# Second layer of an MLP as a Strassen product, in rounds of four feature pairs

## The chip, the cores and the metric

The kernel runs on one core of a Trainium2 chip. The metric is the device time of one execution in microseconds, lower is better, as the median of three runs. One execution was also taken by the hardware profiler; its page and its trace are what is read below.

## The reference

An attention block over 8 x 8 heads gives a matrix of 4352 tokens by 512. Two MLPs follow, one on the result of the other, all in float32:

```
x = attention(x, state)          # 4352 x 512
h = x @ w_in                     # 512 -> 2048
g = where(h >= 1, h, where(h <= -1, 0, (h + 1)**2 / 4))
x = g @ w_out                    # 2048 -> 512
h = x @ w2_in                    # 512 -> 2048
g = max(h, 0) + alpha * min(h, 0)
out = g @ w2_out                 # 2048 -> 512
```

The change concerns the last three lines.

## The kernel before

Every float32 matrix is split in two parts, a high part (a cast on ScalarE, `hi_`, line 73) and a low part (a subtraction on VectorE, `lo_`, line 76). A product of two matrices is three TensorE products, high by high, high by low and low by high.

The first part of the kernel runs the attention and the first MLP together, in 144 steps (nine token tiles by sixteen feature blocks). A table `side` holds, for each step, what else is to be issued there: loads, the decoding of the weights, and the preparation of the second MLP. `decode` takes a weight tile that was loaded as 8-byte numbers and packs it to float32 by one operation on ScalarE and four on VectorE. The decoded `w2_in` goes to memory as it is (`wid`), the decoded `w2_out` as its high and low part (`wod`).

The second MLP is `second()`. The tokens are cut into five superblocks (`HALF`), each of two halves `tk`, the halves 512 tokens wide in the first two superblocks and 384 in the others. Layer 1 takes, for a superblock, two feature blocks at a time (a unit `q`; eight units for a superblock, forty in all). It is a Strassen product (in Winograd's form): the 2 x 2 blocks of features by inner dimension, and of inner dimension by tokens, are multiplied by seven block products instead of eight, `h_item`, line 759, six TensorE products each. Sums of weight blocks (`w_sums`, line 661) and of x blocks (`x_sums`, line 726) are formed before, sums of the results after (`h_after`, line 784). `slope` (lines 768 and 770) then applies the activation. The weights of a unit are fetched raw (`wr_get`, line 646), summed and split again for each superblock.

Layer 2 is the plain product: `o_item`, line 824, one feature block at a time, with g as the stationary operand, 128 tokens of it, and 512 columns of `w2_out` moving. Each token tile of 128 has an accumulator of its own, which takes all sixteen feature blocks, so the result has tokens on its partitions, is copied once and stored by one transfer. `wo_get`, line 744, fetches the split weights of a feature block anew for each half.

The order in `second()` is a merged list: layer-1 products in their order, and a layer-2 item m at place 36 + 1.75 m. `run` and the framework's scheduler turn the program's order into each engine's order; instructions of one engine then run in the order that stands in the program. Tiles come from two pools: U tiles of 2 KB per partition (80 of them) and V tiles of 4 KB (10). PSUM has eight banks, four for accumulators (`pa`) and four for the rest (`pp`). Nearly all loads and stores are issued by the queue of SyncE (SP).

Of the kernel before, what the change touches and what calls it, by code (L numbers as in the profile page):

```python
# [40 lines left out]
def kernel_body(ctx: ExitStack, tc: tile.TileContext, x, state, w1i, w1o, w2i, w2o, alpha, out):  # L41
    nc = tc.nc
    up = ctx.enter_context(tc.tile_pool(name="up", bufs=80))
# [52 lines left out]
    wid = dp.tile([8, 2, 128, 512], F32, name="wid")  # L96
    wod = dp.tile([NF, 128, 1024], F32, name="wod")
# [536 lines left out]
    WR, WU, WB = {}, {}, {}  # L634
# [4 lines left out]
    def w2i_store(j, kh):  # L639
        ld.dma_start(out=wid[j, kh], in_=G.pop(("dec", ("w2i", j, kh))))  # L640

    def wr_get(q):

        for kh in range(2):
            t = U(f"wr{q}{kh}")
            ld.dma_start(out=t, in_=wid[q % 8, kh])
            WR[q, kh] = t

    def parts(t):
        return t.rearrange("p (k e c) -> p k e c", k=2, e=2)  # L650

    def w_sums(q):
        r0, r1 = [parts(WR[q, kh]) for kh in range(2)]
        a11, a21, a12, a22 = r0[:, :, 0], r0[:, :, 1], r1[:, :, 0], r1[:, :, 1]
        sa, sb = U(f"sa{q}"), U(f"sb{q}")
        WR[q, 2], WR[q, 3] = sa, sb
        va, vb = parts(sa), parts(sb)
        s2, s1, s3, s4 = va[:, :, 0], va[:, :, 1], vb[:, :, 0], vb[:, :, 1]
# [5 lines left out]
    def w_split(q, n):  # L664

        t, h = WR.pop((q, n)), U(f"wh{q}{n}", F32R)
        if n == 0:
            t = parts(t)[:, :, 0]
            h, l = [h[:, v * 256:(v + 1) * 256].rearrange("p (k c) -> p k c", k=2) for v in range(2)]
        else:  # L670
            l = U(f"wl{q}{n}", F32R)
        hi_(h, t)
        yield
        yield
        lo_(l, t, h)
        if n == 0:
            WU[q, 0] = h, l
            return
        h, l = parts(h), parts(l)
        for e, k in enumerate({1: (1, 3), 2: (5, 4), 3: (6, 2)}[n]):  # L680
            WU[q, k] = (h[:, :, e], l[:, :, e])

    def pairs(j):
        return 2 * j, 2 * j + 1

    FO = list(range(NF))

    def w2o_put(n):

        raw = G.pop(("dec", ("w2o", FO[n])))  # L690
        h, l = U(f"woh{n}", F32R), U(f"wol{n}", F32R)
        hi_(h, raw)
        WR["o", n] = h, l
        yield
        lo_(l, raw, h)

    def w2o_store(n):
        for e, t in enumerate(WR.pop(("o", n))):
            ld.dma_start(out=wod[FO[n], :, e * 512:(e + 1) * 512], in_=t.bitcast(F32))
# [6 lines left out]
    HO = [0, 5, 4, 6, 1, 2, 3]  # L706
    XR, XB, XT, HB, GT, GR, GS, OA = {}, {}, {}, {}, {}, {}, {}, {}
# [20 lines left out]
    def x_prep(s, step):  # L728

        w = wof(s)  # L730
        n = HO[step]
# [10 lines left out]
    def wo_get(m):  # L742
        t = V(f"wv{m}", F32R)
        ld.dma_start(out=t.bitcast(F32), in_=wod[FO[m % NF]])
        WB["o", m] = t

    def h_item(n):
        q, k = divmod(n, 7)
        s, p = q // 8, HO[k]
        bank = {0: "A", 1: "A", 5: "D", 6: "D", 3: "D", 4: "E", 2: "E"}[p]  # L750
        if p in (0, 5, 4):
            HB[q, bank] = PS(f"hB{q}{p}")
        ps = HB[q, bank][:, :wof(s)]
        wh, wl = WU.pop((q, p))
        m = 0
        for kk in range(2):
            xh, xl = XB[s, p, kk]
            for a, b in ((wh, xh), (wh, xl), (wl, xh)):
                pe.matmul(ps, a[:, kk], b, start=(p in (0, 5, 4) and m == 0), stop=(m == 5),  # L759
                          skip_group_check=True)  # L760
                m += 1

    def slope(q, e, tk, h, g=None):

        s, w = q // 8, wof(q // 8)
        f = pairs(q % 8)[e]
        m = U(f"m{q}{e}{tk}")[:, :w]
        act.activation(out=m, in_=h, func=AF.Relu, scale=-1.0)  # L768
        g = GR[2 * s + tk, f] = m if g is None else g
        dve.scalar_tensor_tensor(out=g, in0=m, scalar=beta_sb[:, f:f + 1], in1=h, op0=ALU.mult, op1=ALU.add)  # L770

    def h_after(n):

        q, k = divmod(n, 7)
        w = wof(q // 8)
        p = HO[k]
        A, D, E = [HB[q, b][:, :w] if (q, b) in HB else None for b in "ADE"]

        def tmp(name):
            GT[q, name] = U(f"{name}_{q}")[:, :w]  # L780
            return GT[q, name]

        def plus(out, a, b):
            dve.tensor_tensor(out=out, in0=a, in1=b, op=ALU.add)  # L784
            return out

        if p == 0:
            act.copy(tmp("p1"), A)
        elif p == 5:
            plus(tmp("u2"), D, GT[q, "p1"])  # L790
        elif p == 1:
            slope(q, 0, 0, A)
        elif p == 6:
            h = plus(tmp("u3"), D, GT[q, "p1"])
            plus(h, E, h)
            slope(q, 1, 1, h, h)
        elif p == 3:
            h = plus(GT[q, "p1"], D, GT[q, "p1"])
            slope(q, 1, 0, h, h)
        elif p == 2:  # L800
            h = plus(GT[q, "u2"], E, GT[q, "u2"])
# [294 lines left out]
```

## Time and profile before

| | |
|---|---|
| median of three runs | 1432.91 us (1432.69 to 1433.84) |
| span of the profiled execution, first to last instruction | 1429.7 us |
| its own time beside the span | not recorded apart; the median of the runs is 3.2 us above the span |
| TensorE, VectorE, ScalarE busy | 98%, 73%, 55% |
| granted TensorE clock | 0.998 of full speed |
| moved by DMA | 253.43 MB, mean 177 GB/s |

Busy time is a sum of instruction times without their overlap. TensorE's instructions are pipelined, so a busy TensorE may still not be at its peak; the distance between the starts of two products tells what one costs. The chain that ended last is followed back from the last instruction, at each step to what released it.

### The profile page before, as it was taken

What the parts mean: (1) busy time and instruction counts of PE and PEld (TensorE: products, weight loads), DVE (VectorE), ACT (ScalarE), POOL (GpSimd) and SP (SyncE); (2) the same over time, 40 slices, a digit from 0 to 9 for tenths busy, and PEclk for the clock granted to TensorE, in tenths of its full rate; (3) what the DMA queues carried; (4) which work ended last, traced back from release to release, by engine and by line L of the source; (5) the groups of instructions that cost most, each with busy time, mean ns of one, the idle gap of its engine ahead of it and who ended that gap; (6) DMA issues with size and microseconds to landing.
All of it is one profiled execution on the core that took longest, in us unless ns stands there. A gap on an engine that the chain in (4) does not pass through costs nothing.

```text
span 1429.7 us, 18991 instructions
## 1 busy us (share of the span) xinstructions
PE 1405.3 (98%) x6548; PEld 1170.0 (82%) x6548; DVE 1044.2 (73%) x1884; ACT 784.4 (55%) x1502; POOL 91.2 (6%) x94
## 2 busy tenths in 40 slices
PE   6799999999999999999999999999999999999998
PEld 4466688888888888888988888888888899989987
DVE  7888685868787888763789786659666976786742
ACT  5566676776776777764644353335433544454431
POOL 1000001121100000000200110002000200010000
PEclk9999999999999999999999999999999999999999
DMA  6898415788744554565323453354545555664545
GB/s 210 309 319 298 119 52 155 212 225 226 216 155 140 162 163 133 163 213 182 120 89 103 155 185 127 125 177 162 177 138 190 201 186 178 201 210 163 184 167 201
DMA packets 146793, 253.43 MB, mean 177 GB/s; under 512 B 47240, under 2 KB 59784, under 8 KB 146696
## 3 DMA queue, kind: packets, MB, share of 16 engines
q1 hardware_dynamic: 107560, 234.54, 49.1%
q0 software_dynamic: 33280, 8.51, 3.2%
q10 hardware_dynamic: 5856, 9.18, 1.7%
q8 instruction: 51, 0.84, 0.3%
q14 instruction: 46, 0.38, 0.1%
HBM read 195.96 MB, written 55.57 MB: 176 GB/s over the span
## 4 chain that ended last, share of the span: by engine, by line
PE 89%; DVE 6%; DMA 2%; ACT 1%; issue 1%; ACTq 0%; SPq 0%; DVEq 0%
PE accB L824 24%; PE accA L613 21%; PE hB L759 21%; PE hA L84 13%; PE accA L605 3%; PE vgp L84 1%; PE sr L84 1%; PE sc L84 1%; DMA vr<-vd 1%; DVE xt L726 1%; DVE gs L76 1%; DMA vd<-vgo 1%; DVE xl L76 1%; PE et L198 0%; DMA wr_wi<-in_moe_w_in_dram 0%
## 5 line engine op out<-in xcount | busy, mean ns | idle before, releaser
L824 PE MATMUL accB<-wv,gs 128*128 128x512 f32 x1632 | 397.2, 391 | 0.0
L824 PEld LDWEIGHTS accB<-wv,gs 128*128 128x128 f32 x1632 | 305.1, 188 | 59.3
L759 PE MATMUL hB<-xh,wh 128*128 128x384 f32 (+1 forms) x640 | 216.9, 359 | 1.0 <-DVE u L784 0.9
L759 PE MATMUL hB<-xl,wh 128*128 128x384 f32 (+1 forms) x560 | 200.2, 357 | 0.0
L759 PE MATMUL hB<-xh,wl 128*128 128x384 f32 (+1 forms) x480 | 170.9, 358 | 0.0
L581 DVE SCALAR_TENSOR_TENSOR g<-y,hA 128x512 f32<-128x512 f32 (+1 forms) x144 | 94.0, 653 | 65.3 <-ACT y L579 64.9
L759 PEld LDWEIGHTS hB<-xh,wh 128*128 128x128 f32 x640 | 119.5, 188 | 17.4 <-DVE u L784 3.3
L578 ACT ACTIVATE y<-hA 128x512 f32<-128x512 f32 (+1 forms) x144 | 82.5, 573 | 87.4 <-PE hA L84 86.1
L768 ACT ACTIVATE m<-u 128x384 f32<-128x384 f32 (+1 forms) x80 | 45.4, 568 | 134.5 <-DVE u L784 134.4
L76 DVE TENSOR_TENSOR gl<-g,gh 128x512 fp32r<-128x512 f32 (+1 forms) x128 | 93.0, 726 | 31.6 <-ACT gh L73 29.7
L759 PEld LDWEIGHTS hB<-xl,wh 128*128 128x128 f32 x560 | 105.1, 188 | 12.6
L76 DVE TENSOR_TENSOR gs<-u,gs 128x384 fp32r<-128x384 f32 (+1 forms) x80 | 48.6, 609 | 72.5 <-ACT gs L73 72.1
L759 PEld LDWEIGHTS hB<-xh,wl 128*128 128x128 f32 x480 | 90.0, 188 | 7.6
L73 ACT CAST gh<-g 128x512 fp32r<-128x512 f32 (+1 forms) x128 | 75.6, 591 | 28.6 <-DVE g L581 26.8
L579 ACT ACTIVATE y<-y 128x512 f32<-128x512 f32 (+1 forms) x144 | 87.6, 608 | 4.3
L73 ACT CAST gs<-u 128x384 fp32r<-128x384 f32 (+1 forms) x80 | 44.4, 556 | 82.0 <-PE accB L824 80.9
L784 DVE TENSOR_TENSOR u<-hB,p 128x384 f32<-128x384 f32 (+1 forms) x80 | 48.5, 607 | 40.9 <-PE hB L759 40.8
L770 DVE SCALAR_TENSOR_TENSOR u<-m,beta_sb,u 128x384 f32<-128x384 f32 (+1 forms) x80 | 56.0, 700 | 25.1 <-ACT m L768 24.2
L605 PE MATMUL accA<-g,wf_w1o 128*128 128x512 f32 x128 | 60.7, 607 | 4.6 <-DVE wf_w1o L398 4.6
L493 ACT COPY vgo<-vgp 128x512 f32<-128x512 f32 x64 | 37.2, 585 | 43.0 <-PE vgp L84 21.9
L76 POOL TENSOR_TENSOR xl<-xr,xh 128x384 fp32r<-128x384 f32 (+1 forms) x15 | 18.4, 1225 | 621.4 <-ACT xh L73 621.4
L73 ACT CAST wh<-sa 128x512 fp32r<-128x512 f32 x40 | 24.8, 621 | 56.7 <-DVE sa L661 51.1
(960 smaller groups left out, 3063.5 us busy)
## 6 DMA issues: line engine op xcount, KB each, us to landing
wv<-wod SPq DMA_DIRECT2D x160, 512.0 KB
wr<-wid SPq DMA_DIRECT2D x80, 256.0 KB
vd<-vgo SPq DMA_DIRECT2D x64, 256.0 KB
x<-in_x_dram SPq DMA_DIRECT2D x30, 512.0 KB
vr<-vd SPq DMA_DIRECT2D x56, 256.0 KB
out_dram<-oB SPq DMA_DIRECT2D x33, 256.0 KB
wr_wi<-in_moe_w_in_dram SPq DMA_DIRECT2D x16, 512.0 KB
wr_w1o<-in_moe_w_out_dram SPq DMA_DIRECT2D x16, 512.0 KB
```

Of the source, the lines that this page charges most:

```text
L73: act.copy(h, raw)
L76: (eng or dve).tensor_tensor(out=l, in0=raw, in1=h.bitcast(F32), op=ALU.subtract)
L84: pe.matmul(ps, a, b, start=(k == 0), stop=(k == n - 1))
L578: act.activation(out=y[:, :n], in_=ps, func=AF.Relu, bias=0.5, scale=0.5)
L579: act.activation(out=y[:, :n], in_=y[:, :n], func=AF.Square)
L581: dve.scalar_tensor_tensor(out=g[:, :n], in0=y[:, :n], scalar=1.0, in1=ps, op0=ALU.min, op1=ALU.max)
L605: pe.matmul(ACC[k], w[:, k * 128:(k + 1) * 128], g, start=(f == 0), stop=(f == NF - 1))
L613: pe.matmul(ACC[k][:, :n], a, b, start=(f == 0 and j == 0), stop=(f == NF - 1 and j == 2))
L759: pe.matmul(ps, a[:, kk], b, start=(p in (0, 5, 4) and m == 0), stop=(m == 5), skip_group_check=True)
L770: dve.scalar_tensor_tensor(out=g, in0=m, scalar=beta_sb[:, f:f + 1], in1=h, op0=ALU.mult, op1=ALU.add)
L784: dve.tensor_tensor(out=out, in0=a, in1=b, op=ALU.add)
L824: pe.matmul(OA[k], a, b, start=(r == 0 and j == 0), stop=(r == NF - 1 and j == 2))
```

## The change

Layer 2 becomes a Strassen product too. A round `r` takes one half superblock of features: four feature pairs `jj` (units 4r to 4r + 3), so two rounds for each superblock, ten in all. For each of the seven products `p` the four pairs are added up in one bank, for each of two column halves `cc` of 128 output features. The weights are now the stationary operand and g moves, 512 or 384 tokens at a time. Three chains of products share the banks: products 0, 5, 6, 3 go on adding in one bank, and after each product the state of the bank is one block of the result and is read out (`o_after`: a copy in the first round, a sum with the copy in the second); 4 and 2 share another, 1 has its own. Layer 1 takes the same chains (`h_item`, `h_after`).

The result stands with output features on the partitions. `o_turn` turns it by 32 x 32 blocks on VectorE, four blocks into one tile, and stores it in pieces of 32 partitions by 4 x 128 columns.

The sums of blocks of g are formed in `o_prep`, in place where possible. The sums of weight blocks of both layers are formed and split once, and stored (`w1c`, 7 products for 8 pairs, and `w2c`): in the first part of the kernel for `w2_in` and for the first two pairs of `w2_out`, and within `second()`, in its first 63 places, for the other six pairs. `second()` fetches one tile for a layer-1 product (`w1_get`, six products ahead) and one V tile for two layer-2 items (`w2_load`, four items ahead). The order: layer-1 products one by one, layer-2 item m at place 34.5 + m. The preparation of x for the next superblock is spread over two units. There are 82 U tiles; the tile `stT` moves from a place of its own to the pool of V tiles.

The core of the diff, of the new side (the old functions stand above):

```diff
-    up = ctx.enter_context(tc.tile_pool(name="up", bufs=80))
+    up = ctx.enter_context(tc.tile_pool(name="up", bufs=82))
...
+    A_CHAIN, B_CHAIN, C_CHAIN = (0, 5, 6, 3), (4, 2), (1,)
+    ORDER = A_CHAIN + B_CHAIN + C_CHAIN
...
+    def w_sums(key, a11, a21, a12, a22, shape):
+        sa, sb = U(f"sa{key[0]}{key[1]}"), U(f"sb{key[0]}{key[1]}")
+        s2, s1, s3, s4 = [shape(t[:, h:h + 256]) for t in (sa, sb) for h in (0, 256)]
...
         for o, a, b, op in ((s1, a21, a22, ALU.add), (s2, s1, a11, ALU.subtract),
                             (s3, a11, a21, ALU.subtract), (s4, a12, s2, ALU.subtract)):
             dve.tensor_tensor(out=o, in0=a, in1=b, op=op)
             yield
...
+    def w_split(key, *products):
+        shape = w1_shape if key[0] == "i" else w2_shape
+        for p in products:
+            src = WS[key].pop(p)
+            t = U(f"ws{key[0]}{key[1]}{p}", F32R)
+            hi_(shape(t[:, :256]), src)
+            yield
+            lo_(shape(t[:, 256:]), src, shape(t[:, :256]))
...
+    L1 = []
+    for q in range(8 * NSUP + 1):
+        for k, (d, p) in enumerate(((0, 0), (1, 4), (0, 5), (1, 2), (0, 6), (1, 1), (0, 3))):
+            if 0 <= q - d < 8 * NSUP:
+                L1.append((q, k, q - d, p))
+    L2 = [(r, p, jj) for r in range(2 * NSUP) for p in ORDER for jj in range(4)]
...
+    def h_after(q, p):
...
+        if p in (0, 5, 6):
+            act.copy(g, ps)
         elif p == 3:
+            slope(q, e, g, ps)
+        else:
+            dve.tensor_tensor(out=g, in0=ps, in1=g, op=ALU.add)
+            slope(q, e, g, g)
...
+    def o_prep(m):
...
+        src = {0: b11, 5: b11, 6: b12, 4: b11, 2: b22, 1: b21}.get(p)
+        if p == 5:
+            dve.tensor_tensor(out=b12, in0=b22, in1=b12, op=ALU.subtract)
+            dve.tensor_tensor(out=b11, in0=b12, in1=b11, op=ALU.add)
+        elif p == 3:
+            src = U(f"t4{q}")[:, :w]
+            dve.tensor_tensor(out=src, in0=b21, in1=b11, op=ALU.subtract)
+        elif p == 4:
+            dve.tensor_tensor(out=b11, in0=b22, in1=b11, op=ALU.subtract)
         v = V(f"gs{m}", F32R)
...
+        hi_(h, src)
+        lo_(l, src, h)
...
     def o_item(m):
+        r, p, jj = L2[m]
...
+        for cc in range(2):
+            if p in (0, 4, 1) and jj == 0:
+                OA[cc, p] = pa.tile([128, 512], F32, tag="acc", name=f"o{r}{p}{cc}")
+            ps = OA[cc, 0 if p in A_CHAIN else 4 if p in B_CHAIN else 1][:, :w]
+            wh, wl = [t[:, h + cc * 128:h + cc * 128 + 128] for h in (0, 256)]
+            for k, (a, b) in enumerate(((wh, gh), (wh, gl), (wl, gh))):
+                pe.matmul(ps, a, b, start=(p in (0, 4, 1) and jj == 0 and k == 0), stop=(jj == 3 and k == 2),
+                          skip_group_check=True)
+            if jj == 3:
+                o_after(r, p, cc, ps)
...
+    def o_after(r, p, cc, ps):
...
+        if p in A_CHAIN and not last:
+            OC[key] = U(f"c{s}{hh}{tk}{cc}")[:, :w]
+            act.copy(OC[key], ps)
+        else:
+            dve.tensor_tensor(out=OC[key], in0=ps, in1=OC[key], op=ALU.add)
+        if last and p in (3, 4, 2, 1):
+            o_turn(s, hh, tk, cc, OC.pop(key))
+
+    def o_turn(s, hh, tk, cc, c):
...
+            dve.transpose(out=o[:, :4 * n].rearrange("p (j k x) -> p k j x", k=4, x=32)[:, k],
+                          in_=c[:, v:v + n].rearrange("p (j t) -> p j t", t=32))
...
+                for i in range(4):
...
+                    ld.dma_start(out=dst[:, :, i * 128:(i + 1) * 128],
+                                 in_=o[32 * i:32 * i + 32, 4 * u:4 * u + 512].rearrange("p (j c) -> p j c", j=4))
...
-        LAG = 36
...
+        LAG = 34.5
+        ev = [(n, 0, n) for n in range(len(L1))] + [(LAG + m, 1, m) for m in range(len(L2))]
+        later = defaultdict(list)
+        for j in range(2, 8):
+            n = 6 + 9 * (j - 2) if j < 4 else 35 + 7 * (j - 4)
+            later[n - 4].append((w2_get, j))
+            later[n].append((w2_sums, j))
+            for k in range(4):
+                later[n + 1 + k].append((w_split, ("o", j), *ORDER[2 * k:2 * k + 2]))
+                later[n + 3 + k].append((w_store, ("o", j), *ORDER[2 * k:2 * k + 2]))
...
+                w1_get(n + AW)
...
+                w2_load(n + 4)
+                o_prep(n + 2)
                 o_item(n)
...
-            at(o + 4, w2i_store, *key[1:])
...
+        elif key[2]:
+            at(o + 2, w1_sums, key[1])
+            for k in range(4):
+                at(o + 3 + k, w_split, ("i", key[1]), *ORDER[2 * k:2 * k + 2])
+                at(o + 5 + k, w_store, ("i", key[1]), *ORDER[2 * k:2 * k + 2])
...
+    AW = 6
...
-    stT["t"] = cp.tile([128, 1024], F32, name="stT")
+    stT["t"] = V("stT")
```

## Rows read from the trace of the kernel before

**Rows 1.** The page's busy times: us, share of the span, instructions.

```profile
PE 1405.3 (98%) x6548; PEld 1170.0 (82%) x6548; DVE 1044.2 (73%) x1884; ACT 784.4 (55%) x1502; POOL 91.2 (6%) x94
```

**Rows 2.** The chain that ended last: start us, us, what; second MLP and end.

```profile
879.13 2.72 PE hB L759 x12
881.85 2.72 PE accB L824 x12
...
1360.54 2.10 PE hB L759 x12
1362.64 2.08 PE accB L824 x9
...
1382.53 42.90 PE accB L824 x189
1425.45 0.38 ACT oB L832
1425.85 0.42 DVE oB L833
```

**Rows 3.** Windows: us, busy of each engine (instructions), TensorE clock, DMA share, GB/s.

```profile
280.00:300.00 20.00, 20.00 (x96) 16.76 (x95) 13.72 (x27) 14.06 (x27) 3.76 (x4) 1.00 0.88 227
...
550.00:600.00 50.00, 50.00 (x237) 41.87 (x236) 45.14 (x87) 34.13 (x66) 0.00 (x0) 1.00 0.40 121
...
765.00:1000.00 235.00, 234.85 (x1040) 194.66 (x1039) 174.58 (x291) 101.89 (x188) 18.76 (x14) 1.00 0.44 150
1000.00:1382.00 382.00, 381.12 (x1883) 340.79 (x1882) 272.35 (x523) 165.39 (x341) 18.25 (x14) 1.00 0.53 180
```

**Rows 4.** Waits of TensorE, 716 us to the end: us, times, longest.

```profile
PE hB L759 <- DVE u L784: 0.9, 4, 0.3
```

**Rows 5.** The page's costliest group: busy us, mean ns, idle before.

```profile
L824 PE MATMUL accB<-wv,gs 128*128 128x512 f32 x1632 | 397.2, 391 | 0.0
```

**Rows 6.** VectorE one by one, 1150 to 1166 us: start, us, instruction, idle before.

```profile
1153.71 0.42 DVE L661 TENSOR_TENSOR sa<-wr,wr 128x256 f32<-128x256 f32 x1
1154.05 0.42 DVE L661 TENSOR_TENSOR sb<-wr 128x256 f32<-128x256 f32 x1
...
1156.10 0.55 DVE L76 TENSOR_TENSOR gs<-u,gs 128x384 fp32r<-128x384 f32 x1
1156.57 0.55 DVE L784 TENSOR_TENSOR u<-hB,p 128x384 f32<-128x384 f32 x1
...
1158.36 0.62 DVE L770 SCALAR_TENSOR_TENSOR u<-m,beta_sb,u 128x384 f32<-128x384 f32 x1 [0.65 <-ACT m L768]
1158.90 0.68 DVE L76 TENSOR_TENSOR wl<-sb,wh 128x512 fp32r<-128x512 f32 x1
1159.50 0.69 DVE L76 TENSOR_TENSOR wl<-wr,wh 128x512 fp32r<-128x512 f32 x1
...
1161.10 0.55 DVE L76 TENSOR_TENSOR gs<-u,gs 128x384 fp32r<-128x384 f32 x1
1161.66 0.56 DVE L784 TENSOR_TENSOR p<-hB,p 128x384 f32<-128x384 f32 x1
1162.14 0.61 DVE L770 SCALAR_TENSOR_TENSOR u<-m,beta_sb,u 128x384 f32<-128x384 f32 x1
```

**Rows 7.** Tiles xsf, xst and wid: min/median/max ns, first and last start in us.

```profile
L292 DVE STREAM_TRANSPOSE xsf<-so x16: 224/236/249, 28.6 to 593.2; 128x64 f32<-128x64 f32 x16
L906 SPq DMA_DIRECT2D xst<-xsf x16: 507/585/620, 579.8 to 600.3; - x16
...
L640 SPq DMA_DIRECT2D wid<-wf_w2i x16: 314/324/424, 264.4 to 452.5; - x16
```

**Rows 8.** DMA issues of the whole span: count, size of one.

```profile
wv<-wod SPq DMA_DIRECT2D x160, 512.0 KB
wr<-wid SPq DMA_DIRECT2D x80, 256.0 KB
```

**Rows 9.** Waits of the sync queue, 716 us to the end: us, times, longest.

```profile
SPq L744 <- PE accB L824: 425.6, 124, 20.4
```

**Rows 10.** The end in order of time: start us, us, what.

```profile
1426.31 0.33 SPq L845 DMA_DIRECT2D out_dram<-oB  x1
```

More of the change, by code (lines that the diff above doesn't have):

```diff
@@ L683, in pairs, with w1_shape @@
[L683 to L699, printed above, removed]
+    def w1_shape(t):
+        return t.rearrange("p (k c) -> p k c", k=2)
@@ new lines, in w2_shape, with w1_sums, w2_get, w2_sums @@
+    def w2_shape(t):
+        return t.rearrange("p (c i x) -> p c i x", c=2, i=4)
+    def w1_sums(j):
+        r0, r1 = [G.pop(("dec", ("w2i", j, kh))).rearrange("p (k e c) -> p k e c", k=2, e=2) for kh in range(2)]
+        return w_sums(("i", j), r0[:, :, 0], r0[:, :, 1], r1[:, :, 0], r1[:, :, 1], w1_shape)
+    def w2_get(j):
+        for e in range(2):
+            t = U(f"wo{j}{e}")
+            ld.dma_start(out=t, in_=wod[2 * j + e])
+            WS["raw", j, e] = t
+    def w2_sums(j):
+        r0, r1 = [WS.pop(("raw", j, e)).rearrange("p (i h c x) -> p h c i x", i=4, h=2, c=2) for e in range(2)]
+        return w_sums(("o", j), r0[:, 0], r0[:, 1], r1[:, 0], r1[:, 1], w2_shape)
@@ new lines, in w_split, with w_store @@
+    def w_split(key, *products):
[6 more added lines that the diff above has]
+            lo_(shape(t[:, 256:]), src, shape(t[:, :256]))
+            WS[key, p] = t
+            yield
+    def w_store(key, *products):
+        for p in products:
+            t = WS.pop((key, p)).bitcast(F32)
+            j = key[1]
+            dst = w1c[j, p] if key[0] == "i" else w2c[p, j // 2, :, j % 2 * 512:(j % 2 + 1) * 512]
+            ld.dma_start(out=dst, in_=t)
@@ L740, in x_prep, with w1_get, w2_load, h_item @@
             XB[s, n, kk] = (h, l)
[L742 to L754, printed above, removed]
+    L1 = []
[4 more added lines that the diff above has]
+    L2 = [(r, p, jj) for r in range(2 * NSUP) for p in ORDER for jj in range(4)]
+    def w1_get(n):
+        if n < len(L1):
+            q, p = L1[n][2:]
+            t = U(f"w1_{q}{p}", F32R)
+            ld.dma_start(out=t.bitcast(F32), in_=w1c[q % 8, p])
+            W1[q, p] = t
+    def w2_load(m):
+        if m < len(L2) and m % 2 == 0:
+            r, p, jj = L2[m]
+            t = V(f"w2_{r}{p}{jj}", F32R)
+            ld.dma_start(out=t.bitcast(F32), in_=w2c[p, r % 2 * 2 + jj // 2])
+            W2[m], W2[m + 1] = t[:, :512], t[:, 512:]
+    def h_item(q, p):
+        s = q // 8
+        w = wof(s)
+        chain = "a" if p in A_CHAIN else "b" if p in B_CHAIN else "c"
+        first = p in (0, 4, 1)
+        if first:
+            HB[q, chain] = PS(f"h{chain}{q}")
+        ps = HB[q, chain][:, :w]
+        t = W1.pop((q, p))
+        wh, wl = w1_shape(t[:, :256]), w1_shape(t[:, 256:])
         m = 0
@@ L768, in slope @@
         act.activation(out=m, in_=h, func=AF.Relu, scale=-1.0)
-        g = GR[2 * s + tk, f] = m if g is None else g
         dve.scalar_tensor_tensor(out=g, in0=m, scalar=beta_sb[:, f:f + 1], in1=h, op0=ALU.mult, op1=ALU.add)
-    def h_after(n):
-        q, k = divmod(n, 7)
+    def h_after(q, p):
         w = wof(q // 8)
[L776 to L796, printed above, removed]
-        elif p == 3:
[L798 to L801, printed above, removed]
-            slope(q, 0, 1, h, h)
```

222 lines of the change are left out of this document (88 added, 134 removed).

## The prediction

> **What bounds the kernel now.** I read the page's busy shares first, then the chain that ended last, then windows by stage, then the waits on TensorE, and last the instructions one by one. TensorE is busy for nearly the whole span and VectorE for 73% [rows 1]. The share alone could hide a slow stage, so the chain: in the second MLP it is TensorE after TensorE, `hB` (layer 1, L759) and `accB` (layer 2, L824) in turn, and it ends with 189 `accB` products in one piece [rows 2]. In the windows of that stage TensorE is busy 234.85 of 235 us and 381.12 of 382 us [rows 3], and the only wait put down to it there is 0.9 us [rows 4]. So the second MLP takes as long as its columns take, and a change pays there by the columns that it removes, as long as nothing else comes to the front.
>
> The price of a column comes from the chain's pieces. 12 products of 512 columns take 2.72 us, 226.7 ns each, in both layers; 12 products of 384 columns take 2.10 us, 175 ns each; 9 `accB` products between them take 2.08 us, 231 ns [rows 2]. Each `hB` product loads its own weights, as layer 2's will, so a stream of 384-wide products is known to run at 175 ns.
>
> **The change, part by part: TensorE.** Layer 2 now does 1632 products of 512 columns [rows 5]: 768 in the 512-wide superblocks (174.1 us) and 864 in the 384-wide ones (199.6 us), 373.7 us. Afterwards each of ten rounds has 7 products x 4 pairs x 2 column halves x 3 = 168 products of the round's width: 672 of 512 (152.3 us) and 1008 of 384 (176.4 us), 328.7 us. Layer 1 keeps its 1680. **Term: -45 us.**
>
> **VectorE in the second MLP.** Issue to issue, a 256-column operation takes 0.335 us, 384 columns 0.47, 512 columns 0.60 [rows 6]. Count a unit, seven products of each layer. At 384 columns TensorE needs 84 x 0.175 = 14.7 us for it (before: 42 x 0.175 + 36 x 0.231 = 15.7). VectorE after the change: 3 sums and 4 slopes of layer 1 (before 5 and 4), 7 low halves for layer 2 (before 4), 4 sums of g, 2.5 sums of output blocks on average (a first round has 6, a last one 14, per four units), 1.9 for the next superblock's x: 22.4 x 0.47 = 10.5 us. The turns come on top. The only narrow one in the trace is 64 columns in 0.24 us [rows 7]; between that and a 256-column sum's 0.335 I take the latter for every piece, 16 pieces in 8 units, 0.7 us. So 11.2 of 14.7 us, 76%. At 512 it is 13.5 + 0.7 = 14.2 of 19.0 us, 75%. What goes are the weight sums and splits, 4 x 0.335 + 0.335 + 3 x 0.60 = 3.5 us a unit. Before, the stage ran at 71 to 74% [rows 3]. The work that covers this is TensorE's own; and 45.14 of 50 us of VectorE went with 50.00 of TensorE in 550 to 600 [rows 3]. I cost it at nothing in the steady state.
>
> It is fuller in two places. In the first four units with layer 2 (round 0) the other weight pairs are summed and split too, 11 x 0.335 = 3.7 us a unit, and where a superblock changes 9 operations (5 us) fall into one unit: 14.2 + 3.7 + 5 = 23 of 19 us. Two items of lookahead (5 us) take most of it; bounds 0 and 4 us for each of four changes. **With what the loads add there, below: +6, bounds 0 and 16.**
>
> **ScalarE** has 7 + 7 + 2 + 1.75 operations a unit at 0.52 us (its 784.4 us over 1502 instructions [rows 1]), 9 of 14.7 us: nothing.
>
> **Loads.** A layer-1 product now has its own load of 256 KB (280, before 80), layer 2 has 140 of 512 KB (before 160) [rows 8]. A 384-wide round (59 us) moves 7.3 + 7.3 + 1.6 MB of weights and data, 275 GB/s; the stage before ran at 180 with the engines busy 0.53, so 340 at full [rows 3], and 275 is 0.81. A 512-wide round moves 16.8 MB in 76 us, 0.65. Round 0 is the exception: it also stores 28 products of 256 KB and fetches 8 raw tiles, with the next x 26.2 MB in 76 us, 344 GB/s, all there is. Leads of six layer-1 products and four layer-2 items (8 to 16 us) and a queue that waited 425.6 us for tiles without harm [rows 9] cover a few us of lateness; this is in the +6 above. On the sync queue a blocked 512 KB load stands ahead of layer 1's loads and of the outputs; the next thing late would be layer 1's weights.
>
> The Trainium skill, "DMA: Bandwidth & Descriptors", section "Specifications", gives the limit of HBM for a core as about 358 GB/s. The 340 of the row lies 5% under it. By 358 round 0 would have 3 us to spare, by the row none; the sum is the same.
>
> **The first MLP.** Removed: 16 low halves and 16 casts of 512 columns. Added: 8 x 11 + 2 x 11 operations of 256 columns on VectorE, 110 x 0.335 - 16 x 0.60 = +27 us, and 70 casts less 16. The larger part, 29 us, falls where the second w_in is decoded; its stores stand at 264 to 452 us [rows 7]. VectorE is at 13.72 of 20 us there [rows 3]; 29 in 190 makes 84%, covered as in 550 to 600. Its 40 further stores (10.5 MB) meet engines that are busy 0.88 in 280 to 300 [rows 3]: about 0.15 more, so full. What is moved there is wanted ten steps and more later; if this cover fails, the split of vr or x1 is late next, and h_mm behind it. **+2, bounds 0 and 10.** stT takes one of the ten V tiles and frees two U tiles: at nothing, the lookahead of loads covers it; bounds 0 and the 10 just named.
>
> **The end.** Before, 189 products ran alone; now the last 31 items do. VectorE in the last round: 28 low halves, 16 sums, 14 output sums at 0.47 and 16 turns, 58 x 0.47 + 5 = 32 us against 28 x 1.05 = 29.5 of TensorE. Four times in it a chain goes on in a bank that must first be read, with 3 products (0.53 us) to cover a sum of 0.55. **+4, bounds 1 and 9.** After the last product came a copy, one issue and the landing, from 1425.43 (1382.53 + 42.90) to 1429.7, 4.3 us [rows 2, 10]. Now: a sum (0.6), two turns (0.6), 12 issues instead of one, landing as before (3.0). An issue takes 0.33 us for the last output [rows 10] and 0.585 for 32-partition pieces, which these are [rows 7]: 4 to 7 us. Sum 8.2 to 11.2. **+5.5, bounds 4 and 7.**
>
> **Sum.** -45 + 6 + 2 + 4 + 5.5 = -27.5. The span of 1429.7 becomes 1402; the median of the runs stands 3.2 us above the span, as what lies around it, so **1405 us**. All terms at their low bounds give 1393, all at the high ones 1430.
>
> **The rivals.**
> *The bank as a new wait.* Layer 2 adds one product to the last in the same bank, and each intermediate state is read out: 10 rounds x 4 hand-overs. If no other product is put in between, each stalls for read-out and two signals less 0.53 us, some 0.7 us: 28 us in place of the 6, and 1427. For it: the 0.9 us that TensorE does wait are of this kind, layer 1 behind L784 [rows 4]. Against it: those are all, though layer 1 has four such hand-overs in each of 40 units, and a layer-1 product (1.05 us) stands between two items. The Trainium skill, "PSUM — Partial Sum Buffer", section "PSUM bank collisions raise a hardware error", has engines kept off one bank by semaphores, so the wait is there in any case; the trace agrees that it is one, with the same 0.9 us.
>
> *Loads bind in round 0 and after.* If the mix with 256 KB loads moves 290 GB/s, round 0 takes 90 us instead of 76, 14 in place of the 6, and the first MLP's full stretch costs its 10: 1421. For it: 227 GB/s at 0.88 in 280 to 300 is 258 at full [rows 3]. Against: that stretch has short packets, this one has not.
>
> *VectorE in order becomes the bound (slower).* If every sum - ScalarE - slope and every sum - cast - low half is waited out, a 384-unit has 4 waits of 0.65 us [rows 6] and 3 of about 0.7 more, and some 0.8 of latency: 11.2 + 5.5 = 16.7 us against 14.7; a 512-unit 20.6 against 19.0. 24 x 2.0 + 16 x 1.6 = 74 us; with -45, 2, 4 and 5.5 that is 1473. It decides against the change from 45 - 11.5 = 33 us of loss on, 0.8 us a unit. For it: the 0.65 wait exists. Against it: the order on VectorE is not the program's; the sum of the next product (1161.66) stands ahead of the slope before it (1162.14), with a low half between [rows 6], so waits are filled.
>
> *No gain.* If two of the first rivals' costs come together the time ends within 0.2%.
>
> **How the numbers follow.** Forecast (1393 to 1415) 0.62; bank waits 0.10; loads 0.13; both and no gain 0.05; VectorE in order 0.10. The range takes in the first three, 1392 to 1428. 0.2% (2.9 us) is about what a measurement of this kernel tells from nothing. Faster 0.86, same 0.04, slower 0.10.
>
> **What would show it.** Right: layer 2 as 1680 products at 227 and 175 ns; TensorE over 98% busy from 765 us to the last layer-1 product; VectorE at 75 to 80% in the 384-wide rounds; DMA near 0.8 there; span 8 to 11 us beyond the last product. Wrong: waits of TensorE on the copies of layer-2 banks by the dozen, or on `w1_` and `w2_` loads in 770 to 860; a VectorE at 95% with TensorE under it; the first `hB` product later than 716 us by more than 3.

## The result, and the profile after

The changed kernel takes 1442.64 us, median of 4 runs (1439.59 to 1443.51), beside 1432.8 for the kernel before on the same chip: a ratio of 1.0066, interval 1.0052 to 1.008. It is slower by 0.66%, where 1405 us and a gain were forecast. The profiled execution has a span of 1441.6 us; before it was 1429.7, so 11.9 us are to be explained (the medians lie 9.8 us apart).

The page of the changed kernel, busy times, the costliest group and an issue line:

```profile
PE 1380.8 (96%) x6596; PEld 1167.1 (81%) x6596; DVE 1110.3 (77%) x2089; ACT 832.5 (58%) x1658; POOL 100.3 (7%) x94
...
L825 PE MATMUL o<-gs,w 128*128 128x384 f32 (+1 forms) x1680 | 378.4, 363 | 17.3 <-DVE gs L76 7.7
...
out_dram<-ot SPq DMA_DIRECT2D x136, 64.0 KB
```

TensorE is busy for 24.5 us less than in [rows 1], and yet the span is longer: it stands idle where it did not. Layer 2 is now 1680 products, as the change says, and it has idle time in front of it (17.3 us) where the group of before had none [rows 5]. The windows of [rows 3] again, and two short ones between them:

```profile
280.00:300.00 20.00, 20.00 (x95) 16.76 (x95) 16.21 (x37) 15.20 (x33) 2.46 (x4) 1.00 0.86 255
...
765.00:1000.00 235.00, 227.42 (x977) 183.86 (x976) 189.71 (x319) 121.45 (x232) 18.23 (x10) 0.99 0.74 255
930.00:960.00 30.00, 26.14 (x107) 20.82 (x106) 18.20 (x34) 10.24 (x19) 0.00 (x0) 0.94 0.74 225
1000.00:1382.00 382.00, 367.93 (x1991) 350.50 (x1990) 294.15 (x573) 182.59 (x393) 26.41 (x18) 0.99 0.73 251
1085.00:1106.00 21.00, 15.40 (x82) 13.91 (x81) 12.70 (x26) 8.03 (x18) 0.00 (x0) 0.99 0.69 205
```

Where TensorE had 234.85 of 235 us it has 227.42, and where it had 381.12 of 382 it has 367.93. The loss sits in short stretches: from 1085 to 1106 it works 15.40 of 21 us, while VectorE (12.70) and the DMA engines (0.69) are less busy than on average. So neither of them is at its limit there; something is late. What TensorE waits for from 716 us on:

```profile
PE o L825 <- DVE gs L76: 7.7, 7, 1.9
PE o L825 <- DMA w<-w2c: 5.0, 2, 3.0
PE hb L766 <- DMA w<-w1c: 2.2, 1, 2.2
PE hb L766 <- DVE g L789: 2.1, 3, 0.8
PE ha L766 <- DMA w<-w1c: 2.0, 2, 1.4
```

In place of one wait of 0.9 us [rows 4] stand waits for weights, for the low halves of the sums of g (`gs`, L76) and for sums of layer 1's results (`g`, L789). The sync queue, which issues every weight load, in order of time from 931 us:

```profile
931.21 7.63 SPq L863 DMA_DIRECT2D out_dram<-ot  x16
938.89 1.39 SPq L742 DMA_DIRECT2D w<-w1c  x3
940.38 0.38 SPq L749 DMA_DIRECT2D w<-w2c  x1
940.85 0.38 SPq L742 DMA_DIRECT2D w<-w1c  x1
942.09 9.40 SPq L863 DMA_DIRECT2D out_dram<-ot  x16
951.53 0.44 SPq L742 DMA_DIRECT2D w<-w1c  x1
```

This is the end of the first superblock: its 32 output stores, 64 KB each, take 17 us of the queue (7.63 us for the first sixteen, 9.40 for the others), and in the 20.3 us from 931.21 to 951.53 the queue issues five loads of weights. A layer-1 product and a layer-2 item take 2.72 us together here, with a load for each product and one for every two items, so TensorE uses up eleven in that time. Not all of it is issuing; the queue's own waits from 930 to 952 us:

```profile
SPq L863 <- DVE ot L850: 2.8, 2, 1.7
SPq L863 <- DMA w<-w1c: 1.1, 2, 0.8
SPq L863 <- DMA w<-w2c: 1.0, 1, 1.0
```

By the profile the stores wait for their turns, and three of them until loads that were issued before them have landed; why a store waits for those isn't shown. The chain of the same kernel from 1345 us shows how that ends:

```profile
1349.34 0.44 SPq L863
...
1350.32 0.03 SPq L749
...
1350.38 3.76 DMA w<-w2c
...
1354.28 3.65 PE o L825 x12
1357.93 1.27 PE hb L766 x6
1359.20 1.04 PE o L825 x6
```

The path runs over store after store (L863), then over the load that stood behind them (L749), 3.76 us of transfer, and only then over TensorE. The twelve products behind it take 304 ns each, those at 1.04 us for six take 173. Two windows of that place (the clock is the third figure from the right) show why:

```profile
1350.00:1354.00 4.00, 2.26 (x13) 1.94 (x12) 3.21 (x8) 2.67 (x7) 0.00 (x0) 1.00 0.81 264
1354.00:1358.00 4.00, 3.72 (x13) 3.75 (x14) 0.37 (x1) 0.80 (x2) 0.00 (x0) 0.61 0.99 361
```

The granted clock is 0.61 on the mean once TensorE has stood, that is, 1.2 GHz for most of those 4 us. And the end, the sync queue from 1400 us:

```profile
1400.84 22.45 SPq L749 DMA_DIRECT2D w<-w2c  x9
1426.95 12.25 SPq L863 DMA_DIRECT2D out_dram<-ot  x24
```

**Where the 11.9 us came from.** I mark three moments: the first layer-1 product of the second MLP, the last product, the end of the span. Between the first two I take each product from its start to the next one's start; what exceeds the regular spacing of its width (226 ns at 512 columns, 173 at 384) by more than 30 ns is a stop, and what exceeds it at the granted clock of 0.5 is put down to the clock (a stop in which the clock falls only at its end is a stop).

| | before | after | difference | forecast |
|---|---|---|---|---|
| start to first layer-1 product | 716.3 | 723.7 | +7.4 | +2 (0 to 10) |
| products at full clock, without stops | 706.3 | 661.2 | -45.1 | -45 |
| stops of TensorE | 2.6 | 38.2 | +35.6 | +6 and +4 (1 to 25) |
| half clock | 0 | 6.4 | +6.4 | none |
| last product to end of span | 4.5 | 12.1 | +7.6 | +5.5 (4 to 7) |

The rows of the column difference add up to 11.9. The first moment is not quite the same place in every kernel: 24 products of the first MLP (2.9 us) come after it in the kernel before, 36 (4.3 us) in the changed one.

### The profile page after: what moved, and what is told of

The parts are those of the page before. It is cut to its first block, busy times and chain, and to the rows that moved or that the text cites. A ratio compares the mean times of both kernels' runs of the same rounds, so it can differ in the third digit from the quotient of the medians.

```text
span 1441.6 us, 20117 instructions
## 1 busy us (share of the span) xinstructions
PE 1380.8 (96%) x6596; PEld 1167.1 (81%) x6596; DVE 1110.3 (77%) x2089; ACT 832.5 (58%) x1658; POOL 100.3 (7%) x94
## 4 chain that ended last, share of the span: by engine, by line
PE 77%; DVE 10%; DMA 8%; issue 2%; ACT 2%; SPq 2%; DVEq 0%; ACTq 0%
PE o L825 20%; PE accA L614 17%; PE ha L766 11%; PE hA L84 11%; PE hb L766 6%; PE accA L606 3%; PE hc L766 3%; DMA w<-w1c 2%; PE vgp L84 1%; DMA x<-in_x_dram 1%; PE sc L84 1%; SPq L863 1%; PE sr L84 1%; DVE gs L76 1%; DVE gl L76 1%
## 5 line engine op out<-in xcount | busy, mean ns | idle before, releaser
L825 PE MATMUL o<-gs,w 128*128 128x384 f32 (+1 forms) x1680 | 378.4, 363 | 17.3 <-DVE gs L76 7.7
L825 PEld LDWEIGHTS o<-gs,w 128*128 128x128 f32 x1680 | 304.1, 190 | 51.2 <-DVE gs L76 13.0
L766 PE MATMUL ha<-xh,w 128*128 128x384 f32 (+1 forms) x640 | 204.4, 360 | 3.4 <-DMA w<-w1c 2.0
L73 ACT CAST gs<-g 128x384 fp32r<-128x384 f32 (+1 forms) x240 | 126.3, 554 | 66.7 <-PE o L825 48.8
L76 DVE TENSOR_TENSOR gs<-g,gs 128x384 fp32r<-128x384 f32 (+1 forms) x240 | 143.7, 624 | 27.0 <-ACT gs L73 26.4
L773 ACT ACTIVATE m<-g 128x384 f32<-128x384 f32 (+1 forms) x120 | 68.2, 568 | 147.1 <-DVE g L789 144.9
L766 PEld LDWEIGHTS ha<-xh,w 128*128 128x128 f32 x640 | 119.6, 189 | 18.6 <-ACT g L785 4.6
L766 PE MATMUL ha<-xl,w 128*128 128x384 f32 (+1 forms) x320 | 114.6, 358 | 0.0
L76 DVE TENSOR_TENSOR gl<-g,gh 128x512 fp32r<-128x512 f32 (+1 forms) x128 | 92.5, 723 | 23.5 <-ACT gh L73 21.8
L785 ACT COPY g<-ha 128x384 f32<-128x384 f32 (+1 forms) x120 | 62.5, 521 | 78.6 <-PE ha L766 77.8
L766 PE MATMUL hb<-xh,w 128*128 128x384 f32 (+1 forms) x320 | 102.1, 359 | 4.3 <-DMA w<-w1c 2.2
L774 DVE SCALAR_TENSOR_TENSOR g<-m,beta_sb,g 128x384 f32<-128x384 f32 (+1 forms) x120 | 82.5, 688 | 17.1 <-ACT m L773 15.4
L789 DVE TENSOR_TENSOR g<-hb,g 128x384 f32<-128x384 f32 (+1 forms) x80 | 48.2, 603 | 54.4 <-PE hb L766 48.6
L839 DVE TENSOR_TENSOR c<-o,c 128x384 f32<-128x384 f32 (+1 forms) x100 | 58.5, 605 | 13.9 <-PE o L825 13.5
L76 POOL TENSOR_TENSOR xl<-xr,xh 128x384 fp32r<-128x384 f32 (+1 forms) x15 | 25.2, 1682 | 625.0 <-ACT xh L73 497.6
```

The costliest lines, as they stand in the source:

```text
L73: act.copy(h, raw)
L76: (eng or dve).tensor_tensor(out=l, in0=raw, in1=h.bitcast(F32), op=ALU.subtract)
L766: pe.matmul(ps, a[:, kk], b, start=(first and m == 0), stop=(m == 5), skip_group_check=True)
L825: pe.matmul(ps, a, b, start=(p in (0, 4, 1) and jj == 0 and k == 0), stop=(jj == 3 and k == 2), skip_group_check=True)
```

## The experiments

The table has what was measured; ratios are to the kernel before, run on the same chip. "First" and "last" are the moments above, "beyond" is from the last product to the end of the span, and stops and half clock are those of the second MLP, all from the one profiled execution.

| kernel | median us | ratio (interval) | first | last | beyond | stops | half clock |
|---|---|---|---|---|---|---|---|
| changed kernel | 1442.64 | 1.0066 (1.0052 to 1.008) | 723.7 | 1429.5 | 12.1 | 38.2 | 6.4 |
| e1_pool_out | 1427.52 | 0.9966 (0.9953 to 0.9978) | 725.7 | 1407.8 | 18.7 | 19.7 | 1.6 |
| e3_no_turn | 1426.96 | 0.9965 (0.9953 to 0.9976) | 725.3 | 1419.2 | 8.3 | 31.2 | 1.6 |
| e4_no_later_prep | 1431.83 | 0.9998 (0.9988 to 1.0009) | 724.3 | 1417.0 | 12.3 | 30.7 | 1.5 |
| e5_raw_w1c | 1446.5 | 1.01 (1.0085 to 1.0115) | 731.6 | 1432.1 | 11.5 | | |
| e6_split_out | 1416.78 | 0.9896 (0.9881 to 0.9911) | 727.5 | 1408.7 | 7.6 | 18.5 | 1.9 |
| e7_store_pool | 1420.97 | 0.9928 (0.9912 to 0.9943) | 730.9 | 1411.6 | 7.9 | | |
| e8_fewer_stores | 1437.49 | 1.0043 (1.0028 to 1.0058) | 722.3 | 1424.8 | 12.5 | | |
| e9_spread_prep | 1411.79 | 0.9867 (0.985 to 0.9883) | 727.5 | 1400.7 | 7.7 | 16.9 | 0 |
| e10_spread_own_stt | 1413.17 | 0.9869 (0.9853 to 0.9885) | 729.4 | 1403.9 | 7.7 | | |
| e11_own_stt | 1439.62 | 1.0057 (1.0039 to 1.0075) | 720.3 | 1425.5 | 12.9 | | |
| e12_before_v_stt | 1436.6 | 1.0033 (1.0022 to 1.0045) | 720.3 | 1428.6 | 4.4 | | |
| e13_neither | 1438.97 | 1.0047 (1.003 to 1.0064) | 717.7 | 1422.1 | 12.7 | 36.7 | 6.7 |

### The output stores off the loads' queue

```diff
-                    ld.dma_start(out=dst[:, :, i * 128:(i + 1) * 128],
+                    pool.dma_start(out=dst[:, :, i * 128:(i + 1) * 128],
```

> The changed kernel, with its 136 output stores issued by GpSimd's queue instead of the sync queue; nothing else differs. Theory A (the sync queue): in the changed kernel 16 stores at about 0.45 us stand in one piece ahead of the weight loads where rounds 2, 4, 6 and 8 begin; without them the stops of TensorE at 940 to 955, 1091 to 1103, 1218 to 1230 and 1341 to 1354 go, with the half clock behind them, and 15 to 20 us are gained (about 1425 us). Theory B (VectorE is too full where a superblock changes): those stops stay, within 3 us of 1442. Theory C (the DMA engines are short of bandwidth): the same packets move, so within 3 us of 1442 as well.

Same data, same sums, same turns; only the engine that issues the 136 stores is another. The time falls by 15.1 us, 1.0% by the ratios. The same two short windows of this kernel:

```profile
930.00:960.00 30.00, 30.00 (x134) 24.86 (x133) 22.78 (x40) 13.60 (x24) 17.45 (x32) 1.00 0.85 274
...
1085.00:1106.00 21.00, 21.00 (x123) 21.00 (x122) 14.54 (x30) 11.21 (x24) 10.20 (x19) 1.00 0.98 357
```

TensorE is full in both (before the edit 26.14 and 15.40), and the DMA engines move more in the same time, 357 instead of 205 GB/s: the bandwidth was there and the loads weren't issued. In the second MLP the stops fall from 38.2 to 19.7 us and the half clock from 6.4 to 1.6. The waits for the low halves (L76) fall too, from 7.7 to 3.7 us, with none of VectorE's work changed, so part of them was probably the late layer-1 weights passed on; no run shows that by itself. Nor were the loads short of tiles that the stores hold: in e1_pool_out six loads of layer-2 weights wait 8.1 us in all for an output tile to be stored, in the changed kernel none does. The Trainium skill, "DMA: Bandwidth & Descriptors", section "Issuing engines are not separate DMA queues", says that issuing from several engines saves only the time that it takes to initiate a transfer, usually small beside the transfer. For one store the run agrees: 0.44 us of the sync queue, beside 4.8 us from issue to landing (median of GpSimd's 136). What counts here is that sixteen stand in a row, with their waits, in front of what TensorE needs, and that was 15 us of the total; how much of it is issue time alone isn't shown. The price of the edit stands at the end, in GpSimd's row from 1405 us:

```profile
1405.50 12.98 POOL L863 DMA_DIRECT2D out_dram<-ot  x24 [72.79 <-DVE ot L850]
```

The 24 last stores take 12.98 us here, and the span ends 18.7 us beyond the last product. Their issue ends 10.7 us beyond it; what fills the other 8.0 us beside the last landing isn't shown.

### Without most of the turning

```diff
+                pool.memset(OT[s, tk, v][0], 0.0)
...
-            dve.transpose(out=o[:, :4 * n].rearrange("p (j k x) -> p k j x", k=4, x=32)[:, k],
-                          in_=c[:, v:v + n].rearrange("p (j t) -> p j t", t=32))
+            dve.transpose(out=o[:, 32 * k:32 * k + 32], in_=c[:, v:v + 32])
```

> The changed kernel without the turning of the results: each piece is turned for its first 32 columns alone and the rest of the output tile is zero, so VectorE is relieved of about 22 us; all stores remain. Theory A (sync queue): the stops at the beginnings of rounds 2, 4, 6 and 8 stay, 1438 to 1442 us. Theory B (VectorE): they shrink, and 12 us or more are gained there, below 1430.

15.7 us less than the changed kernel: the total that theory B gave (below 1430), and far from theory A's. But the edit is not clean. The queue's order changed with it:

```profile
926.36 0.43 SPq L863 DMA_DIRECT2D out_dram<-ot  x1
926.84 0.43 SPq L742 DMA_DIRECT2D w<-w1c  x1
927.31 0.45 SPq L863 DMA_DIRECT2D out_dram<-ot  x1
927.80 0.43 SPq L742 DMA_DIRECT2D w<-w1c  x1
...
932.44 3.75 SPq L863 DMA_DIRECT2D out_dram<-ot  x8
```

Of the 32 stores of this superblock 13 are now issued singly or in twos among the loads, ahead of where the first sixteen stood in one piece. Stops fall by 7.0 us (38.2 to 31.2), the half clock by 4.8, the end by 3.8. So this run doesn't tell the turns from the stores; it fits the burst as the harm, and a shorter chain of turns as the gain at the end.

### Without the sums of layer 2's weights inside the second MLP

```diff
-        for j in range(2, 8):
-            n = 6 + 9 * (j - 2) if j < 4 else 35 + 7 * (j - 4)
+        for j in range(0):
+            n = 0
...
-            ld.dma_start(out=t.bitcast(F32), in_=w2c[p, r % 2 * 2 + jj // 2])
+            ld.dma_start(out=t.bitcast(F32), in_=w2c[p, 0])
```

> The changed kernel without the weight preparation inside the second MLP: pairs 2 to 7 of the second layer are not summed, split or stored, and every load of layer-2 weights takes the first two pairs' place, so 66 operations of VectorE (22 us), 42 casts, 42 stores and 12 loads are left out between layer-1 products 2 and 62. If the stops at 753 to 760 and 829 to 844 us (with the half clock some 9 us) come from that work, 1431 to 1435 us; if from the preparation of the next superblock's x, which stays, 1440 or more.

10.8 us less. The stops around 830 to 845 us (2.06, 0.91 and 1.20 us in the changed kernel) shrink to two of 0.78 and 0.39; those at 934, 943, 1081 and 1092 us, where output stores stand in bursts, stay (1.82, 2.54, 1.97 and 3.22 us). So the two losses are separate. What this removes is VectorE's work and 42 stores and their fetches together; which of the two it is, the run doesn't tell. The changed kernel's chain tells part of it: from 818 to 832 us, before the stop of 2.06, it runs over VectorE alone, while the load that comes late at 755 us (a stop of 1.42) stands behind the sync queue and 5.24 us of transfer. And about 3 of the 10.8 us are half clock at 955 and 1355 us, which this kernel is spared although its stops at those places are as long in sum.

### Both mended

Stores from GpSimd until the last superblock, whose stores ScalarE's and the sync queue share:

```diff
-                    ld.dma_start(out=dst[:, :, i * 128:(i + 1) * 128],
+                    eng = pool if s < NSUP - 1 else (act if i % 2 else ld)
+                    eng.dma_start(out=dst[:, :, i * 128:(i + 1) * 128],
```

> Output stores of the first four superblocks on GpSimd's queue, those of the last one in turn on the sync queue and ScalarE's. With GpSimd alone the last product came at 1407.8 us and the last 24 stores took 13 us of issue behind it (18.7 us to the end). If that end is a matter of issue, 12 issues of about 0.45 us on each of two queues leave 10 us, and the time falls by 8 to about 1419 us; if it is the landing of many 512-byte pieces, it stays within 3 us of 1427.

1416.78: a further 10.7 us, and all of it at the end, which is 7.6 us beyond the last product instead of 18.7. Then, on top of it, the sums of layer 2's weights spread, with four pairs (not two) before the second MLP:

```diff
-        for j in range(2, 8):
-            n = 6 + 9 * (j - 2) if j < 4 else 35 + 7 * (j - 4)
+        for j in range(4, 8):
+            n = 6 + 9 * (j - 4)
...
-    for j in range(2):
-        o = gi(8, 1 + 7 * j)
+    for j in range(4):
+        o = (gi(7, 0), gi(7, 5), gi(7, 10), gi(8, 1))[j]
```

> As e6_split_out, with the sums and splits of four pairs of layer-2 weights in the last third of the first MLP (steps 112 to 129 and 145), where VectorE was about half busy, and the other four at places 6, 15, 24 and 33 of the second MLP, before the next superblock's x is prepared. Leaving this work out gave 11 us. If the collision with the x preparation at 815 to 845 us is what costs, 5 to 8 us of it come back against e6; if the amount of the work or the tiles that it holds cost, within 2 us of e6 or slower.

1411.79, ratio 0.9867: the fastest of all, 1.3% under the kernel before, and nothing of the computation is left out. Beside e6_split_out it is 5.0 us, with intervals that just touch. The second MLP takes 673.2 us (727.5 to 1400.7), where e6_split_out takes 681.2, the changed kernel 705.8 and the kernel before 708.9, and no stretch of it runs at half clock. Of the 8.0 us beside e6_split_out 4.3 are products of the first MLP, which in e9_spread_prep all come before that stretch and not in it; the stops and the half clock fall by 3.5. What TensorE still waits for in it:

```profile
PE o L825 <- DVE gs L76: 3.5, 6, 1.6
PE o L825 <- ACT c L837: 2.3, 3, 1.1
...
PE ha L766 <- DMA w<-w1c: 0.2, 1, 0.2
```

The waits for weights are gone but for 0.2 us.

### Why the second MLP starts later

Seven runs went to the 7 us of the first MLP. First the added work was taken away one part at a time: no sums and splits, with the decoded tile stored seven times in their place; then the stores of the split weights issued from GpSimd (on top of e6_split_out); then one store of seven.

```diff
# e5_raw_w1c
-            at(o + 2, w1_sums, key[1])
...
-                at(o + 3 + k, w_split, ("i", key[1]), *ORDER[2 * k:2 * k + 2])
-                at(o + 5 + k, w_store, ("i", key[1]), *ORDER[2 * k:2 * k + 2])
+                at(o + 5 + k, w_store_raw, key[1], *ORDER[2 * k:2 * k + 2])
# e7_store_pool
-            ld.dma_start(out=dst, in_=t)
+            pool.dma_start(out=dst, in_=t)
# e8_fewer_stores
+            if key[0] == "i" and p:
+                continue
...
-            ld.dma_start(out=t.bitcast(F32), in_=w1c[q % 8, p])
+            ld.dma_start(out=t.bitcast(F32), in_=w1c[q % 8, 0])
```

> The changed kernel without the sums and splits of the first layer's weights in the first MLP: the decoded tile itself is stored seven times for each pair, so the 56 stores remain and 88 operations of VectorE and 56 casts are left out. The first product of the second MLP comes 7.4 us later in the changed kernel than before. Theory D (VectorE and ScalarE are too full in the first MLP): it comes back to within 2 us of 716, and about 6 us are gained. Theory E (the stores themselves, in the sync queue and on the engines that are busy 0.85 there): it stays at 722 or later, and less than 2 us are gained.

> As e6_split_out, and the stores of the summed and split weights on GpSimd's queue as well. Theory E1 (the sync queue, blocked behind stores that wait for VectorE, holds up the loads of x in the first MLP): the first product of the second MLP comes back from 725 to 717 us, and 6 us are gained on e6. Theory E2 (the DMA engines' time): the same bytes move, it stays at 723 or later. GpSimd's own loads of w_in (ws) then stand behind these stores, which may cost some of it.

> The changed kernel with all sums and splits of the first layer's weights, but only one of the seven tiles of a pair stored (8 stores in place of 56) and loaded in place of all seven. VectorE's and ScalarE's work of the first MLP is as in the changed kernel. If VectorE's load is what delays the second MLP by 7.4 us, its first product stays at 723; if the stores are, by queue or by engines, it comes back to within 2 us of 716, and 6 us or more are gained (1436 us).

Without VectorE's added work the first product comes at 731.6, later and not earlier; with the stores on GpSimd at 730.9, later too (727.5 in e6_split_out); with 8 stores for 56 at 722.3, 1.4 us earlier. How sharp such a moment is, the table shows: the changed kernel, e1_pool_out, e3_no_turn, e4_no_later_prep and e6_split_out have one and the same work in the first MLP, and theirs lie from 723.7 to 727.5. So neither the sums alone nor the stores alone can be made out as the cause. Two of these runs can't clear their part either, since the edit brought a stop of its own. The longest wait of TensorE from 280 to 480 us in the changed kernel, in e5_raw_w1c and in e7_store_pool, in this order:

```profile
PE accA L614 <- ACT gh L73: 2.4, 1, 2.4
...
PE accA L614 <- ACT gh L73: 8.6, 2, 8.3
...
PE vgp L510 <- DMA ws<-wd: 7.0, 2, 5.5
```

The 8.3 us stand at 334 us, behind a load of x that is issued between the stores of decoded tiles and takes 12.34 us to land; the 5.5 at 375 us, where GpSimd's own loads of w_in now stand behind the stores. The changed kernel's 2.4 us at 462 are gone in e5_raw_w1c and in e8_fewer_stores. The next suspect was the tile that stT took:

```diff
# e11_own_stt (undone), e10_spread_own_stt (undone in e9_spread_prep); e12_before_v_stt: the reverse, in the kernel before
-    up = ctx.enter_context(tc.tile_pool(name="up", bufs=82))
+    up = ctx.enter_context(tc.tile_pool(name="up", bufs=80))
...
-    stT["t"] = V("stT")
+    stT["t"] = cp.tile([128, 1024], F32, name="stT")
```

> The changed kernel with one thing undone: stT has its own place again and not one of the ten V tiles (the U tiles fall from 82 to 80 to make room). Theory F (the V tile that stT holds makes the loads of x and of the raw weights wait in the first MLP, and that is why the second MLP starts 7 us later): first product of the second MLP at most 718 us after the start instead of 723.7, total 1435 to 1438 us. Rival G (the start comes late from the added sums and stores of the first MLP, whatever place stT has): first product within 2 us of 723.7, total 1440 to 1444.

> The kernel before with this one part of the change done alone: stT in a V tile, 82 U tiles. Theory F: first product of the second MLP at least 721 us after the start instead of 716.3, total 1437 to 1441 us. Rival G: within 2 us of 716.3 and total 1431 to 1434.

> e9_spread_prep (output stores off the queue of the loads, sums of the second layer's weights spread out) with stT in its own place again and 80 U tiles. Theory F: first product of the second MLP at most 721 us after the start instead of 727.5, total 1403 to 1407 us. Rival G: 727.5 within 2 us, total 1410 to 1414.

In the kernel before, the V tile alone costs 4.75 us (interval 3.1 to 6.4) and moves the first product from 716.3 to 720.3: not nothing, as I had put it. But undone in the changed kernel it gives 3.4 us at the first product and a total whose interval overlaps with that of the changed kernel, and undone in e9_spread_prep it gives nothing (1413.17 and 1411.79, first product 729.4). So the tile is a cost where nothing else is late, and not the main one after the change. Last, the two kinds of added work together:

```diff
-            at(o + 2, w1_sums, key[1])
...
+            if p == 0:
+                ld.dma_start(out=w1c[j, p], in_=G["dec", ("w2i", j, 0)])
```

> The changed kernel without the sums and splits of the first layer's weights and with one decoded tile stored for each feature pair (8 tiles instead of 56), which every load then reads: the two added costs of the first MLP, which were taken away one at a time in e5_raw_w1c (seven stores of the decoded tile) and e8_fewer_stores (sums kept), are gone together; stT still holds its V tile. The output isn't the reference's. If the V tile has its share alone and the added work the other (theory F for half): first product of the second MLP 719 to 721.5 us after the start instead of 723.7, as in e12_before_v_stt. If the work is all of it (rival G): 716 to 718. If neither: 723 or later. The total follows the first product: 1442.6 less what it gains, 1435 to 1442.

The first product comes at 717.7, 6.0 us earlier than in the changed kernel and within 1.4 of the kernel before. This is rival G's value (716 to 718). But 36 products of the first MLP come after this moment here and 24 in the kernel before. By a product that stands in one place in all of them, the last one with `w_w1o_0h`, the changed kernel is 8.8 us late (687.6 us for 678.8), e11_own_stt 5.4, e12_before_v_stt 3.9 and e13_neither 2.8. So the V tile's share does appear: e12_before_v_stt and e13_neither, in this order, have their longest wait from 280 to 480 us at the same place, 338 to 339 us, for the exponentials of the attention:

```profile
PE et L198 <- ACT e L190: 2.0, 1, 2.0
...
PE et L199 <- ACT e L191: 2.6, 1, 2.6
```

Some 3 us are the tile's, then, and about 6 the added work's, sums and stores together. These are single executions; kernels with the same first MLP as the changed one scatter from 687.6 to 691.4 at that product. The place of the added work is visible in the chains from 440 to 475 us. In the changed kernel:

```profile
451.56 0.28 DVE wsi L76
451.84 0.61 DVE wf_w2i L399
452.45 0.21 SPq L687
452.76 7.64 DMA x<-in_x_dram
460.42 1.04 ACT x2h L73
461.46 0.56 ACT wf_w2i L382
462.02 0.52 ACT gh L73
462.58 1.21 PE accA L614 x4
```

The load of x is issued behind a store of split weights (L687) that waits for VectorE, takes 7.64 us to land, the cast of x stands ahead of that of `g` on ScalarE, and TensorE waits for `g`. In e13_neither the same stretch is TensorE alone:

```profile
458.89 2.72 PE accA L614 x12
461.61 1.36 PE hA L84 x6
```

It is of the kind that the second MLP shows, a load behind an issue that waits at the head of the sync queue. It needn't be the store: in e4_no_later_prep, with the same first MLP, the chain reaches this load of x over a load of `vr` that takes 12.07 us to land. That it accounts for all of the added work's share isn't shown: this one stop is 2.4 us, and the totals of e13_neither and of the changed kernel (1.003 to 1.0064 and 1.0052 to 1.008) overlap.

## Why the prediction was wrong

**The columns: right.** -45 us forecast, -45.1 measured. Layer 2 alone went from 373.6 to 328.6 us; the small differences in layer 1 (-1.5) and in the products of the first MLP within the stretch (+1.4) cancel.

**VectorE in the steady state: right in kind.** 75 to 76% forecast, 77% in 1000 to 1382; in 765 to 1000, with the sums, 81%. Where no stores stand, TensorE is full beside it.

**"With what the loads add there: +6, bounds 0 and 16", and "+4" for the last round: this step failed.** Together they measured 42 us, 35.6 of stops and 6.4 of half clock, against bounds of 1 to 25. Three things are in it. (1) I counted the 136 stores only after the last product. On the sync queue I named the blocked 512 KB load that "stands ahead of layer 1's loads and of the outputs"; it is the outputs that stand ahead of the loads, 32 of them at the end of a 512-wide superblock and 24 at the end of a 384-wide one, 12 to 17 us of the queue, issue and waits together, against leads of 8 to 16. Moving their issue (e1_pool_out) gave back 18.5 us of stops and 4.8 of half clock. (2) The sums of layer 2's weights inside round 0, which this term was about, cost at most 10.8 us (e4_no_later_prep), about 3 of them half clock outside round 0, within the 16. That VectorE is fuller there was right: the chain before the stop of 2.06 us is VectorE's. (3) Nothing in the trace of before had made TensorE stop in this stage, so a lower clock had no term; 6.4 us came of it.

**"+2" for the first MLP: in its bounds, at 7.4.** It is beyond the 3 us that were named as a sign of being wrong. The sums and stores together make the larger part of it, the V tile the other (e11_own_stt, e12_before_v_stt, e13_neither). "At nothing" for stT was wrong by itself: 4.75 us in e12_before_v_stt.

**"+5.5" for the end: undersized, 7.6.** I counted 12 issues behind the last product. 24 stores come in one burst from 1426.95 on, 12.25 us. The turns that release them, on VectorE:

```profile
1425.96 1.15 DVE L850 STREAM_TRANSPOSE ot<-c 128x256 f32<-128x256 f32 x4
...
1430.13 1.15 DVE L850 STREAM_TRANSPOSE ot<-c 128x256 f32<-128x256 f32 x4
```

The 12 stores of the one half come free 2.5 us before the last product, are being issued until 1433.3, and so stand in front of the 12 that were counted; with two queues the end is 7.6 us (e6_split_out).

**The rivals.** The bank as a new wait: falls, since the waits of layer 1 on copies of its banks (L785) make 1.3 us and those of layer 2 on the sums that read its banks (L839) 1.5. Loads that bind by bandwidth: falls, since e1_pool_out moves 357 GB/s in 1085 to 1106 where the changed kernel moves 205 and stops, and e9_spread_prep moves 383 there, more than the 340 and the 358 that the prediction names. It was near in its place, loads that come late in and after round 0, and wrong in the reason. VectorE in order, as the bound of the stage: falls, at 77% of VectorE and with e9_spread_prep ahead. The outcome on the slower side was none of the rivals; a queue's issue time should have been one, with 136 x 0.44 = 60 us of it on the queue that feeds TensorE.

## What to carry to other kernels

A store on the queue that issues the loads costs its issue time to every load behind it, and its wait as well; what counts is how many come in one piece against the lead of the loads, not their bytes. When a change turns few large stores into many small ones, lay their issue times out on the queue's own timeline at the moment at which they come free, and give them a queue of their own there; at the end, where no load follows, share them between queues. Work that is added to a round with little slack is better spread over the rounds before it than started with it.

## What the hardware showed that I had not expected

After stops of 2 to 3 us the granted clock fell to 0.5 (1.2 GHz), four times in the second MLP of the changed kernel (from about 833, 956, 1106 and 1355 us, behind stops of 2.06, 2.37, 3.14 and 2.19 us), and that cost 6.4 us beside the stops themselves, some 1.6 each time: the twelve products behind the last one take 304 ns each on the mean instead of 173. Not each stop does it: three of 1.02, 0.81 and 1.72 us around 1218 to 1229 didn't, one of 2.54 at 943 in e4_no_later_prep didn't, and one of 2.78 us at 336 in e13_neither didn't either.

A store of 64 KB from 32 partitions holds the sync queue for 0.44 us (median of 136; 0.48 from one to the next in the first burst), a load of 512 KB into 128 partitions for 0.32 (median of 140): the time of an issue doesn't follow the bytes. On GpSimd 24 of these stores take 12.98 us, 0.54 each, no less than on the sync queue.
